# Segment 0 of an attention and MLP block attends whole: new buffers, split TensorE tasks and a new list of work

## The chip, the cores and the metric

One core of a Trainium2 chip runs the whole kernel as one launch. The metric is device microseconds of one execution, median of several. The core's engines run at the same time, each through its own list of instructions in order: TensorE (PE, matmuls and the loads of their weights), VectorE (DVE), ScalarE (ACT), GpSimd (POOL) and SyncE (SP, here the issue of DMAs). They wait for each other by semaphores. PSUM has eight banks of 512 f32 columns for 128 partitions; every matmul writes there and another engine must empty it.

## The reference, cut to what matters

2048 tokens of width 640, 32 heads of 20, four segments of 512 tokens, MLP width 1728. All inputs are bf16.

```python
q, k, v = heads of layernorm(x) @ wq, wk, wv
for s in range(4):                        # segments of 512 tokens
    p = softmax(qs @ ks.T * 20**-0.5 + causal mask)     # inside the segment alone
    a_dot = p @ vs
    a_mem = (phi(qs) @ M) / (phi(qs) @ z + 1e-6)        # phi(t) = t+1 if t>0 else exp(t)
    o = g * a_mem + (1 - g) * a_dot                     # g = sigmoid(beta), one per head
    M += phi(ks).T @ vs;  z += sum(phi(ks))
h  = x + o @ wo
h2 = h + silu(layernorm(h) @ w1) @ w2
```

In segment 0 the memory M is zero, so o is (1 - g) * a_dot there.

## The kernel before, in words

**One hand-written order.** `ORDER` is a list of 1371 task names. `schedule` (L287) walks it: each name may carry an engine (`/A` ACT, `/D` DVE, `/G` POOL, `/S` SP) and buffer slots (`:4`). Every engine executes its tasks in the order of the list; nothing is chosen at run time. A tracker (`Tracker.add`, L79, and `run`, L150) then puts semaphore waits where a task reads or overwrites what another engine wrote. A task whose name begins with `fill` puts so many 128x256 matmuls on zeros into PE's order (L598).

**The work of a segment s.** The names tell the task:

- `n1_st`, `n1_rs`, `n1_ap` (L706 to L723): statistics of a block of 128 tokens on DVE, the inverse deviation on POOL, the normalised block on DVE. In segment 0 the block is transposed by PE (`n1_tp` L732) and copied (`n1_te` L741), later by DMA (`n1_tr`).
- `v` (L774) and its eviction `ve`; `pr` (L808), Q and K of four heads at a time for all 512 tokens in five 128x512 matmuls, and its eviction `qe` (L816); `re_` (L677, L679) once copies wq and wk into the padded layout that `pr` reads. Heads 20 to 31 are spread over the pad rows, and `vt` DMAs gather them into QKV.
- `ex` and `ph` (L823 to L833): phi of Q and K.
- For each of eight groups of four heads: `qk` (L880), score products, four heads at once in four row tiles of 32; `e` (L891), exp of two banks, 128x1024, on ACT, from PSUM into a PT buffer; `mk` (L903), the causal mask of each diagonal block on POOL; `av` (L926), values, four heads at once in four column tiles; `oe`, `tn` (L955, L959), `nm`, `ad`: the memory's part, the transposition back, normalisation.
- `kt`, `mz` (L1048), `ma`, `mb`: the memory for the next segment.
- `ot` (a DMA transpose), `wo` (L1109), `rs`: output projection and residual; `n2_`: second layernorm; `h1` (L1143, the tail of 64 columns L1138), `th` (tanh, L1152), `s` (L1158); `h2` (L1178), `o` (L1195), `out`.

A group of score products covers 1280 columns per head: `a` (key block 0, 512 queries), `b` (blocks 1 and 3, 384 + 128), `e` (block 2 of two groups, 256 + 256). Segment 0 is cut differently: `x` tasks treat its queries 0 to 255 (256 + 128 columns) and `ya`, `yb` its queries 256 to 511, and `wo`, `h1`, `th` and `s` of its first two blocks run before those of the other two, with 256 columns a matmul.

**Buffers.** A `qk` task takes four neighbouring banks of PSUM, slot 0 or 4. PTA, PTB and PTE are pools of two buffers each. xT, hT and oT are one buffer each. Q and K of all segments share one tile QK, so that of segment 1 can be written only where that of segment 0 has been read.

Of the kernel before, what the change touches and what calls it, by code (L numbers as in the profile page):

```python
# [7 lines left out]
BF16 = mybir.dt.bfloat16  # L8
# [219 lines left out]
class Task:  # L228
    __slots__ = ("name", "engs", "emit", "reads", "writes", "prio", "mode", "allocs", "preds", "npred",
                 "succ", "ready", "lat", "start", "end", "eng", "idx", "bw")  # L230
# [4 lines left out]
class Graph:  # L235
# [15 lines left out]
    def task(self, name, engs, emit, reads=(), writes=(), prio=0.0, mode=None, reserve=(), lat=None, bw=0.0):  # L251

        t = Task()
        t.name, t.emit, t.mode, t.lat, t.bw = name, emit, mode, lat, bw
# [32 lines left out]
    def schedule(self):  # L287
# [3 lines left out]
        for row in ORDER:  # L291
# [3 lines left out]
            if name.startswith("fill"):  # L295
                o = owner["ps"][slots[0]]
                assert o is None or o.users == 0
                t = Task()
                a = Alloc("ps")
                a.slot = slots[0]  # L300
                t.name, t.eng, t.emit = "fill", PE, self.filler(a, int(name[4:]))
                order.append(t)
# [3 lines left out]
            t.eng = {"A": AC, "D": DV, "G": PO, "S": SP}[eng] if eng else list(t.engs)[0]  # L306
            assert t.eng in t.engs
# [41 lines left out]
WH = [(0, 0), (0, 1), (1, 0), (1, 1)]  # L349

# [20 lines left out]
n1_ap7:3 epsg1 oe4x/D:0 ve12/D kt02:0 n1_tr7 w_w1_2/S w_w2_0/S kt00:1 w_w1_3/S ex011:0 mk1yb mk5x mt0 qk6x0:4 av0y:2
e6x0:1 e6x2 tn4x:3 oe0y/D:0 av5x:0 tn3x:1 oe5x/A:1 qk7x0:4 e7x2:0 e7x0 nm4x:3 v10:2 nm3x:0 qk2ya0:4 ph041:2
n1_st10:2 ve10/D e2ya0:0 e2ya2 n1_rs11 mta2 mk7x n1_st9:3 n1_rs10 v13:0 mk6x tn0y:2 av7x:3 ve13/D nm0y:1 qk2yb0:4
oe7x/A:0 e2yb2:0 e2yb0 tn5x:3 tn7x:0 nm7x:2 av1y:1 av6x:2 qk3ya0:4 oe6x/D:1 nm5x:3 w_w1_4/S tn6x:2 nm6x:0 ot1:0
w_w2_5/S ot0 w_w2_4/S w_w2_1/S oe1y/A:0 e3ya0:1 e3ya2 ph011:1 pr101:1 mtb3 mz02:2 mk2yb av2y:3 qk3yb0:4 e3yb0:1
e3yb2 ma02/D:0 mz00:2 tn1y:0 oe2y/D:1 n1_ap11:1 qe101/D:0 pr100:3 qk4ya0:4 e4ya0:0 e4ya2 mk3yb ex031:2 nm1y:1
qe100/D wo1:0 av3y:3 qk4yb0:4 e4yb2:0 e4yb0 ma00/D:1 tn2y:2 ex101:1 rs1 wo0:0 oe3y/D:0 n2_st1:5 nm2y:2 kt04:0 tn3y:3
n2_rs1 nm3y:3 rs0 qk5ya0:4 pr140:2 n1_rs8 mk4yb pr121:3 e5ya0:1 e5ya2 qe140/A:0 qk5yb0:4 e5yb2:1 e5yb0 ex140:0
pr141:0 av4y:2 n2_ap1:0 n2_st0:4 n2_rs0 n2_ap0:2 kt01:1 n2_tr1:0 qk6ya0:4 qe141/D mk5yb pr120:1 ph031:0 oe4y/D:1
pr111:0 qe121/D:0 e6ya0:0 e6ya2 qk6yb0:4 qe120/D ex121:2 av5y:3 n2_tr0 h1_0_7_0:1 h1_0_0_0:2 e6yb2:0 e6yb0 qk7ya0:4  # L380
th0_7_0:0 ph101:2 qe111/D:0 oe5y/D:0 tn4y:0 s0_7_0:0 th0_0_0:1 h1_0_8_0:3 nm4y:0 s0_0_0 mz01:1 mz04:0 ma01/D:2
h1_0_3_0:2 e7ya2:1 e7ya0 th0_8_0:0 ma04/D:3 s0_8_0 th0_3_0:1 s0_3_0 tn5y:1 qk7yb0:4 e7yb2:1 mk6yb e7yb0 mk7yb mta0
av6y:0 mtb0 oe6y/A:1 h1_0_12_0:3 h1_0_1_0:2 qk8a0:4 th0_1_0:0 e8a2:0 e8a0 th0_12_0:1 s0_1_0 pr110:0 nm5y:1 qe110/D
h1_0_10_0:2 av7y:1 qk8e0:4 oe7y/D:0 th0_10_0:0 s0_12_0 pr130:0 s0_10_0 e8e2:0 e8e0 h1_0_5_0:2 h1_0_11_0:3 qk8b0:4
th0_5_0:1 n1_ap8:3 qe130/D:0 th0_11_0:0 w_w2_2/S kt03:1 tn7y:0 s0_5_0 nm7y:2 mz03:1 s0_11_0 h1_0_2_0:2 e8b2:0 e8b0
ma03/D:4 h1_0_6_0:0 th0_2_0:1 h1_0_13_0:1 th0_13_0:0 qk9a0:4 pr131:3 s0_2_0 s0_13_0 n1_ap10:0 h1_0_4_0:1 h1_0_9_0:2
qe131/D e9a2:1 e9a0 mk8a mk8e mm0 th0_6_0:1 th0_4_0:0 ex100:1 s0_6_0 mm4 mk8b mm6 qk9b0:4 vt19:0 th0_9_0:1 mm2 mm8
n1_rs9 mtb2 s0_4_0 w_w2_3/S vt16 vt10 vt18 e9b2:1 e9b0 av8:3 h2_0_0:0 h2_0_1 qk10a0:4 s0_9_0 ph100:0 ex141:1 ph121:1
e10a2:0 e10a0 h2_0_2 tn6y:2 h2_0_3 ph141:0 ex120:2 mk9a qk10b0:4 oe8/D:0 nm6y:3 o0 mzc0 mzc6 ph120:0 mzc2 h2_1_0:2
mk9b mm10 mzc4 e10b0:0 kt10:0 vt15 mm1 mzc1 mb00:0 e10b2 mk10a mzc5 mzc8 mm7 mzc7 mb03:0 mk10b ex111:1 n1_tr10:0  # L390
tn8:0 vt11 n1_tr8 nm8:0,0 h2_1_1 vt13 ot2 ot3 qk10e0:4 ph111:2 vt111 kt12:1 vt17 vt110 vt12 h2_1_2 av9:0 h2_1_3
ex110:2 ph110:0 oe9/D:1 e10e0:1 e10e2 qk11a0:4 mk10e mm3 mzc3 mb01:0 wo3:0 ad8:0 n1_ap9:2 o1 n1_tr9 vt14 e11a2:1
n1_tr11 e11a0 ex131:1 av10:2 mk11a mzc10 qk11b0:4 e11b0:1 e11b2 mk11b mb02:0 mm9 mzc9 rs3 oe10/D:0 tn9:0 wo2:2
qk12a0:4 nm9:1,1 v20:0 rs2 n2_st3:6 ex130:2 ph130:0 e12a2:0 e12a0 av11:2 qk13a0:4 n2_st2:7 mz12:3 ma12 ve20/A:0
e13a2:1 e13a0 v21:0 mz10:3 qk12b0:4 ve21/A e12b2:0 e12b0 ma10 tn10:0 pr210:3 n2_rs3 qk12e0:4 ph131:1 ad9 mm11 mzc11
mb04:0 mk13a n2_rs2 mk12b mk12a nm10:2,0 e12e2:0 pr220:0 n2_ap3:0 oe11/D:1 qe210/D:0 pr231:1 qe220/D:0 e12e0 mk12e
# [57 lines left out]
def build(nc, es, A_x, A_wq, A_wk, A_wv, A_wo, A_beta, B_x, B_w1, B_w2, out):  # L454
# [397 lines left out]
    def declare_ticks(s):  # L852
# [403 lines left out]
```

## Time and profile before

| | |
|---|---|
| median of three runs | 306.54 us (306.52 to 307.28) |
| span of the profiled execution | 305.4 us |
| busy PE, ACT, DVE, POOL | 291.0, 227.0, 218.7, 143.5 us |
| last matmul ends | 302.76 us |
| moved by DMA | 24.65 MB |

The page of the profile lists these for one execution. Lines that begin with an engine and a line of the kernel are groups: what is written and read, the shapes, how often, and the idle time of that engine before them with what ended it. A line of the timeline has the start, the duration, and then the group. A line of waits has who waited for whom, the total in us, how often, and the longest. A line of stages has the stretch, its length, and the busy time of PE, of PE's weight loads, of DVE, ACT and POOL (instructions in brackets), then granted clock, DMA share and GB/s.

### The profile page before, as it was taken

The page shows a single profiled execution, that of the slowest core. Times are in us where ns is not written, and L with a number is a line of the kernel's source. Part 1 is how long each engine was busy: PE and PEld are TensorE (multiplying, and loading weights), DVE is VectorE, ACT ScalarE, POOL GpSimd, SP SyncE. Part 2 cuts the span into 40 slices and gives each one's busy share as a digit, 9 for nine tenths or more (in the row PEclk, how much of TensorE's full clock was granted, in tenths as well). Part 3 has the DMA queues.
Part 4 walks back from the last instruction along what each step waited for, and adds up shares of the span by engine and source line. Part 5 has one row for each costly group of instructions (what it writes and reads, how often), then busy time and mean ns, then how long its engine had stood idle before and what let it go on. Part 6 is the DMA issues. An engine that isn't in the chain of part 4 may idle for free.

```text
span 305.4 us, 7240 instructions
## 1 busy us (share of the span) xinstructions
PE 291.0 (95%) x2876; PEld 166.5 (55%) x2900; DVE 218.7 (72%) x490; ACT 227.0 (74%) x322; POOL 143.5 (47%) x280
## 2 busy tenths in 40 slices
PE   8699898999999999999999999999999999999996
PEld 6434454555655445656654444556564466764574
DVE  5567999796788895877989878449776476934523
ACT  4488998999998979989889899978878951004410
POOL 4227754433687856536747419334973730300000
PEclk9899999999999999999999999999999999999999
DMA  6658468642264040055552400034250004242001
GB/s 197 211 195 239 75 166 223 127 97 42 90 105 80 17 62 2 1 91 76 114 146 63 67 17 19 2 64 69 39 108 2 0 2 88 64 88 86 0 24 64
DMA packets 48578, 24.65 MB, mean 81 GB/s; under 512 B 38881, under 2 KB 47457, under 8 KB 48545
## 3 DMA queue, kind: packets, MB, share of 16 engines
q1 hardware_dynamic: 47872, 23.09, 33.1%
q10 hardware_dynamic: 672, 1.10, 1.1%
q8 instruction: 23, 0.38, 0.5%
q14 instruction: 11, 0.08, 0.1%
HBM read 10.41 MB, written 2.62 MB: 43 GB/s over the span
## 4 chain that ended last, share of the span: by engine, by line
PE 72%; ACT 12%; DVE 7%; DMA 4%; issue 2%; POOL 1%; SPq 1%; DVEq 0%; ACTq 0%
PE ps_all L1178 18%; PE ps_all L1143 16%; PE ps_all L808 12%; PE ps_all L1109 7%; PE ps_all L880 6%; PE ps_all L926 5%; ACT PTA L891 4%; ACT PTB L891 3%; DMA sT<-in_A_wq_dram 3%; PE ps_all L774 2%; PE ps_all L955 2%; ACT PTE L891 2%; DMA oT<-otok 1%; PE ps_all L959 1%; PE ps_all L1048 1%
## 5 line engine op out<-in xcount | busy, mean ns | idle before, releaser
L891 ACT ACTIVATE PTA<-ps_all 128x1024 bf16<-128x1024 f32 x64 | 62.1, 1027 | 7.1 <-PE ps_all L880 6.5
L1178 PE MATMUL ps_all<-w_sb,sT 128*128 128x320 bf16 x448 | 65.2, 299 | 0.0
L891 ACT ACTIVATE PTB<-ps_all 128x1024 bf16<-128x1024 f32 (+1 forms) x64 | 58.9, 970 | 5.9 <-PE ps_all L880 5.6
L1143 PE MATMUL ps_all<-hT,w_sb 128*128 128x512 bf16 (+1 forms) x315 | 60.1, 335 | 0.9 <-issue 0.5
L1152 ACT ACTIVATE th<-ps_all 128x512 f32<-128x512 f32 (+2 forms) x70 | 34.0, 507 | 34.5 <-PE ps_all L1143 26.8
L1158 DVE SCALAR_TENSOR_TENSOR sT<-th,ps_all 128x512 bf16<-128x512 f32 (+2 forms) x70 | 38.0, 561 | 26.1 <-ACT th L1152 25.0
L903 POOL TENSOR_SCALAR_AFFINE_SELECT PTB<-PTB 128x512 bf16<-128x512 bf16 x64 | 41.2, 644 | 32.7 <-ACT PTB L891 30.4
L1178 PEld LDWEIGHTS ps_all<-w_sb,sT 128*128 128x128 bf16 x448 | 42.3, 98 | 19.3 <-issue 2.1
L1143 PEld LDWEIGHTS ps_all<-hT,w_sb 128*128 128x128 bf16 x325 | 30.3, 98 | 23.9 <-issue 1.3
L891 ACT ACTIVATE PTE<-ps_all 128x1024 bf16<-128x1024 f32 (+1 forms) x40 | 35.4, 943 | 2.2 <-PE ps_all L880 2.1
L903 POOL TENSOR_SCALAR_AFFINE_SELECT PTE<-PTE 128x512 bf16<-128x512 bf16 x40 | 25.9, 647 | 21.0 <-ACT PTE L891 19.5
L706 DVE BATCH_NORM_STATS2 stt<-x_tok 128x6 f32<-128x320 bf16 x64 | 27.9, 477 | 1.5 <-DMA x_tok<-in_A_x_dram 1.3
L808 PE MATMUL ps_all<-xT,wqr 128*128 128x512 bf16 x92 | 24.3, 391 | 3.2 <-ACT xT L741 2.4
L1109 PE MATMUL ps_all<-wo_sb,oT 128*128 128x320 bf16 x160 | 24.1, 299 | 1.0 <-DMA oT<-otok 0.7
L774 PE MATMUL ps_all<-wv_sb,xT 128*128 128x320 bf16 x160 | 24.3, 300 | 0.7 <-DMA xT<-xn_rot 0.5
L808 PE MATMUL ps_all<-xT,wkr 128*128 128x512 bf16 x94 | 24.0, 386 | 0.5 <-issue 0.3
L1000 POOL TENSOR_TENSOR otok<-on 128x320 bf16<-128x320 bf16 x24 | 19.0, 792 | 11.3 <-DVE on L992 11.3
L903 POOL TENSOR_SCALAR_AFFINE_SELECT PTA<-PTA 128x512 bf16<-128x512 bf16 x24 | 15.5, 645 | 16.6 <-ACT PTA L891 16.4
L1195 DVE SCALAR_TENSOR_TENSOR x_tok<-ps_all,x_tok 128x640 bf16<-128x640 f32 (+1 forms) x17 | 13.2, 780 | 14.1 <-PE ps_all L1178 14.0
L880 PE MATMUL ps_all<-QK 20*128 20x256 bf16 (+3 forms) x360 | 20.5, 286 | 1.7 <-ACT PTB L891 0.7
L992 DVE TENSOR_TENSOR on<-ps_all,rd 128x640 bf16<-128x640 f32 x24 | 19.8, 825 | 0.8
L817 DVE CAST QK<-ps_all 128x512 bf16<-128x512 f32 x24 | 16.3, 687 | 5.5 <-PE ps_all L808 5.1
(79 smaller groups left out, 403.5 us busy)
## 6 DMA issues: line engine op xcount, KB each, us to landing
out_dram<-x_tok SPq DMA_DIRECT2D x15, 160.0 KB, 1.9
w_sb<-in_B_w_dram SPq DMA_DIRECT2D x4, 432.0 KB, 5.8
w_sb<-in_B_w_dram SPq DMA_DIRECT2D x3, 480.0 KB, 4.3
x_tok<-in_A_x_dram SPq DMA_DIRECT2D x2, 640.0 KB, 4.7
QKV<-QK SPq DMA_DIRECT2D x16, 72.0 KB
wv_sb<-in_A_wv_dram SPq DMA_DIRECT2D x1, 800.0 KB, 4.9
sT<-in_A_wq_dram SPq DMA_DIRECT2D x1, 800.0 KB, 8.2
sT<-in_A_wk_dram SPq DMA_DIRECT2D x1, 800.0 KB, 9.9
```

The costliest lines, as they stand in the source:

```text
L706: T.add(DV, lambda e, hh=hh: e.bn_stats(out=stt[:, s, 6 * hh:6 * hh + 6], in_=xb[:, 320 * hh:320 * hh + 320]), reads=R((xa, xsub)), writes ...
L774: fns.append(lambda e, c=c, hh=hh: e.matmul(bank(ps, hh)[:, 0:320], lhsT=xT[:, c, 128 * i:128 * i + 128], rhs=wv_sb[:, c, 320 * hh:320 * h ...
L808: fns = [lambda e, kc=kc: e.matmul(bank(ps)[:, lo:hi], lhsT=wt[:, kc, c, :], rhs=xT[:, kc, lo:hi], start=(kc == 0), stop=(kc == NC - 1)) f ...
L880: fns.append(lambda e, j=j, o=o, r=r, q0=q0, q1=q1, qa=qa, ka=ka: e.matmul(ps_all[:, o:o + q1 - q0], lhsT=ka[32 * r:32 * r + DH, 128 * j:1 ...
L891: T.add(AC, lambda e: e.activation(out=pt[:, pta.slot, q0:q0 + 2, 0:width], in_=sc3[:, b0:b0 + 2, 0:width], func=ACT.Exp, scale=SCALE), re ...
L903: fns.append(lambda e, v=v: e.affine_select(out=v, in_=v, pattern=[[0, 4], [1, 128]], compare_op=ALU.is_ge, fill=0.0, base=0, channel_mult ...
L992: T.add(DV, lambda e: e.tensor_tensor(out=on[:, ona.slot, :, :].rearrange("p b (x e) -> p b x e", e=DH), in0=v[:, :, :, 0:DH], in1=r2.unsq ...
L1109: fns.append(lambda e, c=c, hh=hh: e.matmul(bank(ps, hh)[:, 0:320], lhsT=oT[:, c, 128 * i:128 * i + 128], rhs=wo_sb[:, c, 320 * hh:320 * h ...
L1143: fns = [lambda e, c=c: e.matmul(bank(ps)[:, lo:hi], lhsT=w1_sb[:, c, 128 * f:128 * f + 128], rhs=hT[:, c, lo:hi], start=(c == 0), stop=(c ...
L1152: T.add(AC, lambda e: e.activation(out=th[:, tha.slot, lo:hi], in_=bank(ps)[:, lo:hi], func=ACT.Tanh, scale=0.5), reads=R((ps, [0])), writ ...
L1158: T.add(DV, lambda e: e.scalar_tensor_tensor(out=sT[:, f, lo:hi], in0=th[:, tha.slot, lo:hi], scalar=1.0, in1=bank(ps)[:, lo:hi], op0=ALU. ...
L1178: fns.append(lambda e, f=f, t0=t0, fr=fr, hh=hh: e.matmul(bank(ps, hh)[:, 0:320], lhsT=sT[:, f, t0:t0 + 128], rhs=w2_sb[:, fr, 320 * hh:32 ...
```

## The change

The whole list is new. Beside it:

- Segment 0 has `a`, `b` and `e` score tasks like the other segments, one `av`, `oe`, `tn` and `nm` per group, and one set of `h1`, `th` and `s` for its 512 tokens.
- A `qk` task takes two pairs of banks, each anywhere in PSUM.
- One pool PT of seven buffers stands for PTA, PTB and PTE; one pool T of three for xT, hT and oT.
- Q and K of segment 0 lie in the space of w2 (rows 0 to 7 of `w2_sb`), so that parts 0 to 2 of w2 are loaded only after they have been read.
- `v`, `wo`, `pr` and `h1` are two tasks each (`.0` and `.1`); `ph` is `pa` and `pb`. `re_` may run on POOL.
- A PE task could also run as four column tiles of 32 (`/C`); no entry of the list asks for it. The tail of `h1` is always in four tiles of 32 columns.

The diff, cut:

```diff
-        "x": 12, "xn": 4, "xT": 1, "hT": 1, "wq": 1, "wk": 1, "wv": 1, "wo": 1, "w1": 1, "w2": 1,
+        "x": 12, "xn": 4, "T": 3, "wq": 1, "wk": 1, "wv": 1, "wo": 1, "w1": 1, "w2": 1,
+        "QZ0": 1, "QZ1": 1, "QZ2": 1, "QZ3": 1, "QZ4": 1,
-        "PTA": 2, "PTB": 2, "PTE": 2, "oTs": 2, "on": 2, "rd": 4, "otok": 1, "oT": 1,
+        "PT": 7, "oTs": 2, "on": 2, "rd": 4, "otok": 1,
...
+    QK0 = w2_sb[:, 0:8, :].rearrange("p f e -> p (f e)").rearrange("p (c w t) -> p c w t", c=5, w=2)
...
+    def mms(eng, out, lhsT, rhs, start, stop):
+        if eng != "cols":
+            return [lambda e: e.matmul(out, lhsT=lhsT, rhs=rhs, start=start, stop=stop)]
+        return [lambda e, p=p: e.matmul(out[p:p + 32, :], lhsT=lhsT[:, p:p + 32], rhs=rhs, start=start, stop=stop,
+                                        tile_position=(0, p)) for p in (0, 32, 64, 96)]
...
-            G.task(f"re_{k}{c}", {DV: 0.36 if c < 3 else 0.42, AC: 0.72}, emit, rr, ww, prio + c)
+            G.task(f"re_{k}{c}", {DV: 0.36 if c < 3 else 0.42, AC: 0.72, PO: 0.8 if c < 3 else 0.9}, emit, rr, ww, prio + c)
...
-                sca = G.alloc("ps", nr)
+                sca = [G.alloc("ps", 2) for _ in range(nr // 2)]
...
-        if s == 0:
-            for g in range(NG):
-                k = P["x0"] + P["xs"] * g
-                pe = scores(f"{g}x", "PTE", PTE, [(g, 0, 0, 256, 0), (g, 1, 128, 256, 256)], k, 384,
-                            [(0, 0), (1, 0)])
...
+        pe = None
+        for g in range(NG):
+            k = k0 + g
+            pa = scores(f"{k}a", "PT", PT, [(g, 0, 0, L, 0)], k)
+            pb = scores(f"{k}b", "PT", PT, [(g, 1, 128, L, 0), (g, 3, 384, L, 384)], k + P["qkp"])
...
-        parts = [(0, 2), (2, 4)] if s == 0 else [(0, 4)]
+        parts = [(0, 4)]
...
+    def load_w2():
+        for k, (f0, f1) in enumerate(((0, 4), (4, 7), (7, 10), (10, 13))):
+            old = [(a, WH) for a in segs[0]["qk"]] if k < 3 else []
+            load_w(f"w2_{k}", w2_sb[:, f0:f1, :], cw(B_w2[128 * f0:128 * f1, :]), 2 + k, 0.45 * (f1 - f0),
+                   [(W["w2"], [k])] + old)
```

The head of the two lists:

```diff
-n1_rs1 epsg0 n1_ap0:0 fill21:0 n1_tp0:0 n1_te0/A:0 n1_ap1:1 fill6:2 n1_tp1:2 n1_te1/A v00:0 v01:2 n1_st2:2 n1_rs2
-n1_st3:3 n1_rs3 mt1 mt2 mta1 n1_ap2:2 n1_ap3:3 n1_tp2:4 n1_te2/D re_wq1/A:0 fill4:6 n1_tp3:6 n1_te3/A pr010:6
+n1_st1:6 n1_rs1 sel n1_ap0:3 mtb1 fill42:0 n1_tp0:3 n1_ap1:3 fill5:0 n1_tp1:6 w_k n1_st2:4 n1_rs2 n1_te0/A:1 n1_st3:0
+beta n1_rs3 re_wq3/G:0 v00.0:0 v00.1 n1_ap2:3 n1_te1/A v01.0:6 ve00/A:0 mm1 mm5 fill3:4 n1_tp2:2 re_wk1/G:0 n1_te2/A
+v01.1 n1_ap3:1 n1_tp3:0 v02.0:4 v02.1 n1_te3/A re_wq0/D pr000.0:0 pr000.1 ve02/A v03.0:3 re_wk0/D mt2 re_wq4/A
```

More of the change, by code (lines that the diff above doesn't have):

```diff
@@ L229 @@
     __slots__ = ("name", "engs", "emit", "reads", "writes", "prio", "mode", "allocs", "preds", "npred",
[L230 removed]
+                 "succ", "ready", "lat", "start", "end", "eng", "idx", "bw", "cols", "alt")
 class Graph:
@@ L305, in schedule @@
             assert not any(self.tasks[p].name in todo for p in t.preds), name
-            t.eng = {"A": AC, "D": DV, "G": PO, "S": SP}[eng] if eng else list(t.engs)[0]
-            assert t.eng in t.engs
+            t.cols = eng == "C"
+            t.eng = {"A": AC, "D": DV, "G": PO, "S": SP, "C": PE}[eng] if eng else list(t.engs)[0]
+            assert t.eng in t.engs and (t.alt or not t.cols)
             for a in t.allocs:
@@ L822, in e_ex @@
                     def e_ex(eng, c=c, w=w, exa=exa, wall=wall):
-                        T.add(AC, lambda e: e.activation(out=ex[:, exa.slot, :], in_=QK[:, c, w, :], func=ACT.Exp),
+                        T.add(AC, lambda e: e.activation(out=ex[:, exa.slot, :], in_=qkt[:, c, w, :], func=ACT.Exp),
                               reads=R((qk[c], wall)), writes=R((exa, [0])))
```

375 lines of the change are left out of this document (185 added, 190 removed).

## The prediction

> **What bounds the kernel now.** I read the page's busy table and its slices first.
>
> ```profile
> PE 291.0 (95%) x2876; PEld 166.5 (55%) x2900; DVE 218.7 (72%) x490; ACT 227.0 (74%) x322; POOL 143.5 (47%) x280
> ...
> PE   8699898999999999999999999999999999999996
> ...
> ACT  4488998999998979989889899978878951004410
> ...
> PEclk9899999999999999999999999999999999999999
> ```
>
> TensorE (PE) is busy in 291.0 of 305.4 us, so there are three ways to gain: less PE work, fewer waits of PE, a better start. ScalarE (ACT) is nearly as full until about slice 31. Then the timeline of PE, which starts each group of matmuls:
>
> ```profile
> 1.12 4.66 PE L599 MATMUL ps_all<-zpad 128*128 128x256 bf16 x21 [1.12 <-DVE zpad L578]
> 5.69 0.72 PE L732 MATMUL ps_all<-ident,xn_rot 128*128 128x128 bf16 x5
> 6.20 0.91 PE L599 MATMUL ps_all<-zpad 128*128 128x256 bf16 x6
> ...
> 13.77 1.91 PE L808 MATMUL ps_all<-xT,wqr 128*128 128x512 bf16 x4 [2.38 <-ACT xT L741]
> 15.48 2.89 PE L808 MATMUL ps_all<-xT,wkr 128*128 128x512 bf16 x10
> 18.30 0.34 PE L880 MATMUL ps_all<-QK 20*128 20x256 bf16 x8
> 18.57 1.25 PE L808 MATMUL ps_all<-xT,wqr 128*128 128x512 bf16 x5
> 19.66 1.24 PE L808 MATMUL ps_all<-xT,wkr 128*128 128x512 bf16 x5
> 20.84 0.34 PE L880 MATMUL ps_all<-QK 20*128 20x256 bf16 x8
> 21.11 1.25 PE L808 MATMUL ps_all<-xT,wqr 128*128 128x512 bf16 x5
> ```
>
> Starts tell what a group costs. Five 512-column matmuls take 1.09 us from start to start (18.57 to 19.66), a plain stream of 0.216 us each. From 19.66 to 20.84 it is 1.18, and the eight score products behind take 0.27 where their two rounds of 256 and 128 columns are 0.165 at that rate. So each change between full-array matmuls and matmuls in row or column tiles costs PE about 0.10 us. Elsewhere single matmuls start 0.136 us apart at 320 columns, 0.109 at 256, 0.056 at 128. The start is slow: 21 fillers take 0.213 us each, half speed, the clock is full from 6.4 us, PE idles 2.38 us, and then seven projection matmuls run at half speed again.
>
> The waits of PE, and the stages, with busy times:
>
> ```profile
> PE ps_all L808 <- ACT xT L741: 2.4, 1, 2.4
> ...
> PE ps_all L880 <- ACT PTB L891: 0.7, 2, 0.5
> PE ps_all L1109 <- DMA oT<-otok: 0.7, 1, 0.7
> PE ps_all L926 <- POOL PTB L903: 0.6, 1, 0.6
> ...
> 18.30:71.00 52.70, 49.28 (x605) 26.13 (x609) 43.70 (x118) 49.08 (x72) 27.23 (x55) 1.00 0.60 153
> 71.00:127.00 56.00, 54.32 (x620) 30.92 (x625) 44.47 (x100) 52.08 (x73) 37.74 (x78) 1.00 0.28 52
> ```
>
> No single wait is large after the start. The stages are cut at the first score product (18.3), the first of segment 1 (71.0, qk8a0) and of segment 2 (127.0, qk16a0).
>
> **PE's work, counted.** I took the PE order of both built programs and priced each matmul (one round of four tiles counts once) by its start-to-start time, and each change of tiling by 0.10:
>
> - before: 261.8 us of stream, 217 changes; after: 263.8 us, 199 changes.
> - Stream: 61 fillers instead of 41, +2.2. The rest falls by 0.2: h1 of segment 0 has 65 products of 512 columns for 130 of 256. Score and value columns are the same (1280 per group and product kind), only in fewer, wider groups; the tail of h1 keeps its columns. Its tiles are 32 columns wide instead of 64: L926 already runs four such tiles in a round, so 0, within 0.1 us either way for all tails.
> - Changes of tiling: 18 fewer, -1.8.
>
> Splitting PE tasks in two, the free choice of PSUM pairs, seven shared PT buffers, three shared T buffers and Q/K of segment 0 in w2's space add no instruction; they act through waits. The split of phi in two tasks keeps both VectorE (DVE) operations.
>
> **The start.** Before, real work by 18.3 us is 20 v matmuls (2.7), 15 projections (3.2) and transposes (1.1). After, the list puts all 40 v matmuls there (5.4), 10 projections (2.2) and the transposes: 8.7 instead of 7.1. When does its first score start? The 42 fillers begin at 1.12; 24 at 0.213 to 6.3 us, 18 at 0.109: they end at 8.2. Before, the transpose could start at 5.69. It matters here because ap1 now writes the same xn buffer (3) as ap0 and so waits on DVE for the first transpose; behind it on DVE stand the statistics of blocks 2 and 3. From 8.2, with the durations of before: transpose to 8.5, ap1 to 9.2, statistics of blocks 2 and 3 to 11.35 (two times 1.05), rstd on GpSimd (POOL), ap3 to 12.9, fourth transpose to 13.2, v02 to 14.6, then pr000, half of v03, pr001 and the other half to 18.1, the eviction, and the first score at 18.4. So 1.6 us more work done 0.1 later: **-1.5**. The 2.4 us idle and the second half-speed stretch go; 2.5 us of that are eaten by the fillers. Bounds: fillers all at half speed end at 10.1 (+1.9 on this); at best the first transpose starts where it did, at 5.69 (-2.5).
>
> Here a rule bears on it. The trace went to full clock 5.2 us after the first matmul. The Trainium skill, "TensorE: Matmul & The Clock Gate", Part 1, puts the warm-up at a time budget of about 3.4 us in a free-running window, not a number of matmuls; by it the fillers would end near 7.4, an estimate, and the sum would be 0.8 lower. It also puts the fall back to half rate after an idle window of that length, while this trace shows it after 2.38 us; there the measurement decides.
>
> Five weight rearrangements move to POOL. No row shows them; the nearest are L1084 (168 to 252 elements, 179 ns more: 2.1 ns an element, 1.35 us for 640) and DVE's own copies (0.36 us). I take 1.35, the row on the same engine. wk lands at about 14.1, so re_wk1 ends at 15.5, and its projection comes only after the first score at 18.4. This 3 us of cover makes it 0; without it the cost would be up to 1 us.
>
> **After the start: waits.** Own execution before: 18.3 to the first score; PE work 47.6, 53.7 and 172.3 in the three stages; the last matmul ends at 302.76, the span 2.65 later. So waits are 305.4 - 2.65 - 18.3 - 273.6 = 10.9: 5.1, 2.3 and 3.5 by stage. For other engines I multiplied the instructions that the list has in a stage by their start-to-start times (exp of 1024: 0.905; ex 0.52; th 0.494; evictions 0.49 to 0.74; mask 0.594):
>
> - first score to qk8a0: before PE 47.6, ACT 46.7, DVE 42.0, POOL 27.9; after **PE 38.0, ACT 40.3, DVE 37.6**, POOL 30.0
> - to qk16a0: before 53.7, 49.3, 41.1; after 52.0, 49.1, 42.8
> - to the end: before 172.3, 110.7; after 180.2, 105.5.
>
> So the new list runs segment 0 with three engines level. Cut finer (some 20 pieces between score products), the fullest engine exceeds PE by 5.5 us in sum, where before it was 4.1: +1.4. Against it, score products before used banks 4 to 7 alone until segment 2 and could start only when both exps of the last had ended; a new one needs only two free pairs, so PE can refill one pair while ACT reads another. PE's waits for exps (L891) in the list of waits come to 1.7, most of it there. I set the two against each other: **0**, with -5.4 (waits only where another engine is fuller) and +5 as ends.
>
> Loads of w2: parts 0 to 2 wait until Q/K of segment 0 are read, and parts 1 and 2 each for the landing of the part before, on SP. At 5.8 us each they land by about 121 us, and h2_0_2 stands near 127: covered. Behind them on SP stands kt20, with some 2 us to spare; gone, that costs 1 to 2 us, inside the +5.
>
> **Sum** on the span: 18.4 + 38.0 + 52.0 + 180.2 + 10.9 + 2.65 = 302.1, that is -3.3 (1.5 from the start, 2.0 from stream and changes, less 0.1 for one later filler and rounding). The median lies 1.1 above the span, so 306.5 - 3.3 = **303.2 us**.
>
> **Rivals.**
>
> - *ACT becomes the bound of the first 90 us.* Before, ACT stood idle 52.7 - 46.7 = 6.0 us in the first stage and 56.0 - 49.3 = 6.7 in the second. If it still idles so long, the stages last 40.3 + 6.0 and 49.1 + 6.7, PE waits 12.1 there instead of 7.4, and the time is 303.2 + 4.7 = 307.9: slower. For it: ACT alone exceeds PE in stage one. Against: the looser pairs. My forecast has ACT idle 8.0 us in both stages; from 11.3 on the gain is gone.
> - *The loose buffers do all they can*: waits fall to the 5.5 us of unequal load: 303.2 - 5.4 = 297.8. Against: semaphore latencies remain.
> - *The fillers eat the start* (the change does not bring its earlier start): all 42 at half speed, 305.1.
> - *The clock rises earlier*: if it is full after 16 fillers of 0.213 us instead of 24, the other 26 at 0.109 end at 7.4: 302.4. The trace's 5.2 us speak against it. The rule of the Trainium skill named above is this case.
>
> **Chances.** Forecast 0.38, ACT the bound 0.27, loose buffers 0.15, fillers 0.10, earlier clock 0.10. A measurement of this kernel tells about 0.3% (0.9 us) from no change. Faster: 0.31 + 0.15 + 0.06 + 0.08 = 0.60; within: 0.07 + 0.05 + 0.04 + 0.02 = 0.18; slower: 0.22, all from ACT. The range runs from 299.5 to 308.5: it leaves out half of the loose-buffer case and the worst of ACT's. The sign of faster holds most of the chance; its own range is 300.5 to 305.5.
>
> **What would show it.** In the profile after: the filler group from 1.12 to about 8.2 and the first score near 18.4 (the start); no half-speed projections around 14 us; PE's waits for exps small and its waits between first score and qk16a0 near 7.4; starts of segment 1 and 2 near 61.5 and 116; ACT idle 8 us in these stages. Wrong would be: many waits of score products for ACT or of value products for POOL in the first 110 us, ACT idle there 11 us or more, or long waits for transposes in the last 170.

## The result and the profile after

| | before | after |
|---|---|---|
| median, seven runs each | 305.82 us (304.96 to 307.28) | 303.46 us (301.99 to 304.82) |
| span of the profiled execution | 305.4 us | 301.8 us (time 303.53) |
| first score product | 18.3 | 17.96 us |
| first score product of segment 1, of segment 2 | 71.0, 127.0 | 61.2, 115.4 us |
| last matmul ends | 302.76 | 298.89 us |
| waits of PE by stage (stage less counted PE work) | 5.1, 2.3, 3.5 | 5.2, 2.2, 3.3 us |

The ratio is 0.992, 95% interval 0.990 to 0.994: faster by 0.8%. The span of the profiled execution is 3.6 us shorter. The ratios of three experiments below (x2 and x3 first; both; both sets of fillers) leave out executions over 1.5% longer than the fastest of the same kernel, and in the first and the last of them the profiled execution is such a one.

The page of the changed kernel, the lines that stand first in the prediction:

```profile
PE 291.5 (97%) x2757; PEld 158.8 (53%) x2757; DVE 222.8 (74%) x465; ACT 213.6 (71%) x275; POOL 148.3 (49%) x292
...
PE   8999789999999999999999999999999999999996
...
ACT  3589898999899999966769967868888741004400
...
PEclk9999999999999999999999999999999999999999
```

PE is as busy as before in a shorter span. The 6 that PE had from 7.6 to 15.3 us is gone; one thin place is left, a 7 and an 8 between 30 and 45 us. The timeline of PE at the start:

```profile
1.13 6.38 PE L614 MATMUL ps_all<-zpad 128*128 128x256 bf16 x42 [1.13 <-DVE zpad L593]
7.34 0.44 PE L745 MATMUL ps_all<-ident,xn_rot 128*128 128x128 bf16 x5
...
14.27 1.24 PE L544 MATMUL ps_all<-tT,wqr 128*128 128x512 bf16 x5
15.35 0.84 PE L544 MATMUL ps_all<-wv_sb,tT 128*128 128x320 bf16 x5
...
17.96 0.40 PE L899 MATMUL ps_all<-w_sb 20*128 20x512 bf16 x4
```

The fillers end at 7.3, no projection runs at half speed (five in 1.08 us, 14.27 to 15.35), and there is no idle time of 2.4 us. The longest waits of PE, and the stages cut at the same events as before (the last row runs 0.3 us beyond the last matmul):

```profile
PE ps_all L899 <- DVE otok L995: 1.1, 2, 0.9
...
PE ps_all L544 <- DMA tT<-otok: 0.7, 1, 0.7
...
PE ps_all L980 <- DVE oTs L962: 0.5, 1, 0.5
PE ps_all L947 <- DVE Mz L1085: 0.5, 1, 0.5
PE ps_all L980 <- ACT PT L912: 0.4, 1, 0.4
```

```profile
17.96:61.20 43.24, 39.47 (x415) 17.51 (x415) 39.75 (x92) 40.99 (x50) 31.41 (x70) 1.00 0.58 142
61.20:115.40 54.20, 53.26 (x532) 26.04 (x532) 46.19 (x96) 51.16 (x65) 31.63 (x59) 1.00 0.42 93
115.40:299.20 183.80, 182.28 (x1699) 103.82 (x1698) 126.95 (x251) 112.69 (x148) 75.12 (x127) 1.00 0.24 51
```

The order of the list is new: VectorE stands at its head, and no score product waits long for an exp (L912). In the first stage DVE is busy 39.75 of 43.24 us, ACT 40.99, PE 39.47. With the counted work of ACT (40.3 and 49.1) it idles 2.9 and 5.1 us in the first two stages, together 8.0.

### The profile page after: what moved, and what is told of

It reads as the page before. It is cut to its first block, busy times and chain, and to the rows that moved or that the text cites. A ratio compares the mean times of both kernels' runs of the same rounds, so it can differ in the third digit from the quotient of the medians.

```text
span 301.8 us, 6943 instructions
## 1 busy us (share of the span) xinstructions
PE 291.5 (97%) x2757; PEld 158.8 (53%) x2757; DVE 222.8 (74%) x465; ACT 213.6 (71%) x275; POOL 148.3 (49%) x292
## 4 chain that ended last, share of the span: by engine, by line
PE 76%; DVE 10%; DMA 5%; ACT 2%; SPq 2%; issue 2%; POOL 1%; DVEq 0%
PE ps_all L544 58%; PE ps_all L899 7%; PE ps_all L947 5%; DMA x_tok<-in_A_x_dram 2%; DVE stt L719 2%; PE ps_all L976 2%; ACT PT L912 2%; DMA tT<-otok 2%; PE ps_all L980 2%; DMA tT<-xn_rot 1%; PE ps_all L1056 1%; SPq L1109 1%; DVE w_sb L830 1%; PE ps_all L1146 1%; DVE xn_rot L736 1%
## 5 line engine op out<-in xcount | busy, mean ns | idle before, releaser
L912 ACT ACTIVATE PT<-ps_all 128x1024 bf16<-128x1024 f32 x160 | 154.4, 1031 | 24.9 <-PE ps_all L899 23.3
L924 POOL TENSOR_SCALAR_AFFINE_SELECT PT<-PT 128x512 bf16<-128x512 bf16 x128 | 82.3, 648 | 70.7 <-ACT PT L912 67.1
L544 PE MATMUL ps_all<-w_sb,sT 128*128 128x320 bf16 x448 | 65.7, 299 | 0.1
L544 PE MATMUL ps_all<-tT,w_sb 128*128 128x512 bf16 x260 | 62.6, 380 | 0.3 <-issue 0.3
L1159 ACT ACTIVATE th<-ps_all 128x512 f32<-128x512 f32 (+1 forms) x56 | 31.7, 587 | 37.2 <-PE ps_all L544 26.9
L544 PEld LDWEIGHTS ps_all<-w_sb,sT 128*128 128x128 bf16 x448 | 42.6, 98 | 19.7 <-issue 2.4
L1165 DVE SCALAR_TENSOR_TENSOR sT<-th,ps_all 128x512 bf16<-128x512 f32 (+1 forms) x56 | 36.4, 663 | 20.7 <-ACT th L1159 20.4
L544 PEld LDWEIGHTS ps_all<-tT,w_sb 128*128 128x128 bf16 x260 | 23.2, 98 | 27.6 <-issue 3.6
L544 PE MATMUL ps_all<-tT,wqr 128*128 128x512 bf16 x100 | 25.8, 381 | 0.5 <-DMA tT<-xn_rot 0.5
L544 PE MATMUL ps_all<-tT,wkr 128*128 128x512 bf16 x100 | 25.3, 380 | 0.0
L544 PE MATMUL ps_all<-wv_sb,tT 128*128 128x320 bf16 x160 | 24.9, 299 | 0.0
L544 PE MATMUL ps_all<-wo_sb,tT 128*128 128x320 bf16 x160 | 23.8, 299 | 0.7 <-DMA tT<-otok 0.7
L728 POOL TENSOR_TENSOR rst<-mvt,eps_c 128x1 f32<-128x1 f32 x32 | 6.7, 210 | 28.5 <-DVE mvt L722 28.4
L730 POOL TENSOR_TENSOR rst<-rst,eps_c 128x1 f32<-128x1 f32 x32 | 18.3, 572 | 2.5
L544 PEld LDWEIGHTS ps_all<-wo_sb,tT 128*128 128x128 bf16 x160 | 15.0, 98 | 7.8 <-issue 1.1
```

Source lines behind the costliest of these rows:

```text
L544: return [lambda e: e.matmul(out, lhsT=lhsT, rhs=rhs, start=start, stop=stop)]
L912: T.add(AC, lambda e: e.activation(out=pt[:, pta.slot, q0:q0 + 2, 0:width], in_=sc3[:, b0:b0 + 2, 0:width], func=ACT.Exp, scale=SCALE), re ...
L924: fns.append(lambda e, v=v: e.affine_select(out=v, in_=v, pattern=[[0, 4], [1, 128]], compare_op=ALU.is_ge, fill=0.0, base=0, channel_mult ...
L1159: T.add(AC, lambda e: e.activation(out=th[:, tha.slot, lo:hi], in_=bank(ps)[:, lo:hi], func=ACT.Tanh, scale=0.5), reads=R((ps, [0])), writ ...
L1165: T.add(DV, lambda e: e.scalar_tensor_tensor(out=sT[:, f, lo:hi], in0=th[:, tha.slot, lo:hi], scalar=1.0, in1=bank(ps)[:, lo:hi], op0=ALU. ...
```

## Experiments

The theory after the result: the gain is PE's smaller work and the fuller start, and the waits stay equal only because the loose pairs pay for running three engines level. What is left is (a) the fillers and the landing of x2 at the start and (b) VectorE's lateness from 28 to 37 us. The rivals: other engines are as full in (b), or the clock decides.

**The changed kernel once more**

> The changed kernel once more, unaltered, on the chip of the next three runs, so that they can be compared with it. Every theory expects a ratio to the kernel before of 0.992 within 0.002, a span near 301.8 us and the first score product near 18.0 us.

Median 303.85 us, ratio 0.9932 (0.9908 to 0.9955), first score 18.49, span 302.1. One thing differs from the first profile. A table by stretch (its last columns are granted clock, DMA share, GB/s), first of this execution, then of the first one:

```profile
33.00:37.00 4.00, 2.33 (x43) 1.24 (x36) 3.70 (x12) 3.49 (x5) 1.70 (x4) 1.00 0.37 73
37.00:41.00 4.00, 4.00 (x31) 2.04 (x33) 2.63 (x7) 3.34 (x5) 3.59 (x9) 0.57 0.39 81
```

```profile
33.00:37.00 4.00, 2.33 (x31) 1.35 (x30) 3.47 (x12) 3.49 (x5) 2.24 (x5) 1.00 0.33 62
37.00:41.00 4.00, 3.80 (x48) 2.09 (x46) 3.93 (x11) 3.83 (x5) 3.58 (x9) 1.00 0.39 82
```

PE works 2.33 of the 4 us from 33 to 37 in both. In the one, the clock then falls to 0.57; five value projections take 1.39 us instead of 0.84. By the mean clock of each execution (0.994 against 0.999 or 1.0), 8 of 12 executions of the changed kernel have such a fall, and 2 of 17 of the kernel before that were run beside this one. The last section shows what differs between the two. The means are 303.9 us for those 8 and 302.9 for the other 4: about 1 us.

**Half of the fillers**

```diff
-mtb1 fill42:0 n1_tp0:3
+mtb1 fill21:0 n1_tp0:3
```

> Only edit: 21 fillers instead of 42 ahead of the first transpose. Theory: the fillers cost the start nothing, because in the changed kernel VectorE takes up the statistics of block 2 only at 8.73 us, when the DMA of x2 has landed, and that DMA does not know of the fillers. Then the first score product stays within 0.4 us of 17.96, the ratio within 0.002 of the unaltered changed kernel, and if the clock falls in the longer idle time the start is even up to 1 us later. Rival (the prediction's own chain, in which the transposes wait for the fillers and everything behind them waits for the transposes): the fillers end about 2 us earlier, and the first score comes 1 to 2 us earlier, the span 1 to 2 us shorter.

```profile
1.13 3.78 PE L614 MATMUL ps_all<-zpad 128*128 128x256 bf16 x21 [1.13 <-DVE zpad L593]
5.59 0.45 PE L745 MATMUL ps_all<-ident,xn_rot 128*128 128x128 bf16 x5 [0.68 <-DVE xn_rot L736]
...
6.97 0.89 DVE L719 BATCH_NORM_STATS2 stt<-x_tok 128x6 f32<-128x320 bf16 x2 [0.33 <-DMA x_tok<-in_A_x_dram]
...
16.20 0.40 PE L899 MATMUL ps_all<-w_sb 20*128 20x512 bf16 x4
```

Theory and rival each hold in part. In the 11 profiles with this order of work at the start the first score comes 9.22 or 9.23 us after VectorE takes up the statistics of block 2. These start at the later of two events: the landing of x2, and the end of the second normalised block, which waits for the first transpose and so for the fillers. In this run the landing decides (6.95 us). In the unaltered run beside it x2 has landed at 8.42, and VectorE is held by the transpose:

```profile
8.90 0.45 DVE L736 TENSOR_SCALAR xn_rot<-x_tok,mvt,rst 128x640 bf16<-128x640 bf16 x1 [3.21 <-PE ps_all L745]
9.26 0.88 DVE L719 BATCH_NORM_STATS2 stt<-x_tok 128x6 f32<-128x320 bf16 x2
```

So of the 2.3 us between the two first scores (16.20 and 18.49) 0.8 are the fillers' and 1.5 an earlier landing. In the first profile x2 landed at 8.70 and the fillers cost nothing, as the theory says; over the nine profiles with 42 fillers they hold the statistics 0 to 2.0 us beyond the landing, 0.8 in the mean. In all three profiles with 21 fillers the landing decides: 6.95, 7.81 and 8.91 us, and first scores at 16.20, 17.06 and 18.16. The 2.3 us hold up to segment 1 (60.01 against 62.34); 1.46 are left at segment 2 and at the last matmul. Ratio 0.9902 (0.9871 to 0.9933): 0.3% below the unaltered kernel, with intervals that overlap, so a gain is not shown.

**x2 and x3 ahead of wv**

```diff
-x1:1 w_wv:0 halfc x2:2 x3:3 w_q:0
+x1:1 halfc x2:2 x3:3 w_wv:0 w_q:0
-fill42:0 n1_tp0:3 n1_ap1:3
+fill21:0 n1_tp0:3 n1_ap1:0
```

> Three edits at the start: 21 fillers instead of 42, a buffer of its own for the second normalised block (no wait for the first transpose), and the loads of x2 and x3 issued ahead of that of wv. Theory: the landing of x2 at 8.7 us ends the chain in front of the first score; issued ahead of the 800 KB of wv it lands 2 to 3 us earlier, the statistics of blocks 2 and 3 follow block 1 on VectorE at once, and the first score moves from 17.96 towards 16.5, where the landing of wk at 13.6 holds it (wk's landing, rearrangement, five projection products 1.25, eviction 0.6): a span 1 to 1.5 us shorter, a ratio 0.003 to 0.005 lower than that of the unaltered changed kernel. Rival A: the 13.6 us of wk alone set the start, or the stage behind is held by VectorE and takes the gain back: within 0.5 us. Rival B: the fillers were what held it: then the run with 21 fillers alone has the same gain.

```profile
10.42 4.16 PE L544 MATMUL ps_all<-wv_sb,tT 128*128 128x320 bf16 x15 [3.16 <-DMA wv_sb<-in_A_wv_dram]
14.37 0.85 PE L614 MATMUL ps_all<-zpad 128*128 128x256 bf16 x3
```

A miss that the theory had not named. The statistics of block 2 do follow at once (6.66), but wv is now what lands last: PE waits 3.16 us for it, the clock falls, and 15 value projections take 4.0 us from start to start instead of 2.0. The first score comes at 21.95. Ratio 0.9945 (0.9915 to 0.9975), executions from 301.8 to 308.2 us; the profiled one, at 308.19, is among the longest, and the shortest has a mean clock of 1.0 against its 0.983.

**Statistics of segment 2 later**

```diff
-n1_st9 n1_rs9 (behind e3a0)  n1_st11 (behind ma02)  n1_st10 (behind e4b2)
+n1_st9 n1_rs9 n1_st11 n1_st10 (all behind qk5a0)
```

> Only edit: the statistics of blocks 9, 10 and 11 (three times 1.05 us on VectorE) stand behind qk5a0 in the list instead of ahead of it. Theory: PE's waits from 21 to 41 us come from VectorE, which carries more than PE there (the chain of waits runs over VectorE from 21.7 to 40.6 us); with some 3 us less of work ahead of 41 us PE waits 1.5 to 2.5 us less in the first stage, segment 1 begins at 59 to 60 instead of 61.2, and the span is 1 to 2.5 us shorter. Rival 1 (the prediction's): exp on ScalarE is the bound there; then nothing moves, within 0.4 us. Rival 2: the time is only moved, and VectorE is late in the second half of the stage instead: segment 1 begins within 0.5 us of 61.2.

Slower, 1.0086 (1.0062 to 1.011), where 1 to 2.5 us of gain were expected. Up to qk4a0 nothing moves (41.62 against 41.55): the statistics of block 9 stood behind 37 us, so the edit took nothing from the stretch in which DVE is late. Then qk5a0 to qk6a0 take 3.4 us longer. The timeline of POOL and PE's list of waits from 18 to 63 us show why:

```profile
49.41 0.19 POOL L728 TENSOR_TENSOR rst<-mvt,eps_c 128x1 f32<-128x1 f32 x1 [4.25 <-DVE mvt L722]
49.67 0.55 POOL L730 TENSOR_TENSOR rst<-rst,eps_c 128x1 f32<-128x1 f32 x1
50.19 1.34 POOL L924 TENSOR_SCALAR_AFFINE_SELECT PT<-PT 128x512 bf16<-128x512 bf16 x2
```

```profile
PE ps_all L947 <- POOL PT L924: 3.3, 1, 3.3
```

POOL takes the inverse deviation of block 9 in the list's order, waits 4.25 us for its statistics, and the masks queued behind it are late for the value products. The moved step's second instruction, on another engine, is the larger part of the cost. A second fall of the clock, from 54.4 to 57.9 us, lies in the piece behind it, qk6a0 to qk7a0, which takes 7.7 us instead of 6.35.

**VectorE relieved in the right place**

```diff
-n1_st7 (behind pr030.0)  n1_rs7 n1_ap7 (behind oe0)  n1_st6 n1_rs6 (behind e2e0)
+n1_st7 (behind nm1)  n1_rs7 n1_st6 (behind e3a0)  n1_ap7 n1_rs6 (behind e3b0)
-n1_ap6 (behind e3b0)  n1_st9 n1_rs9 (behind e3a0)  n1_st11 (behind ma02)  n1_st10 (behind e4b2)
+n1_ap6 (behind ve10)  n1_st9 (behind ma02)  n1_rs9 (behind ve11)  n1_st11 (behind e4b2)  n1_st10 (behind qe110)
```

> Edit: the statistics of blocks 7, 6, 9, 11 and 10 on VectorE are each put one place later in the list (block 7 behind the second normalisation of segment 0, block 6 where block 9 was, and so on, block 10 behind the eviction of the second projection of segment 1), and the inverse deviations on GpSimd and the normalised blocks with them, each behind its own statistics and ahead of nothing that waits longer. So VectorE has 2.1 us less to do ahead of 36 us. Theory: PE waits for VectorE between 28 and 37 us (0.3, 0.3, 0.9 and 0.5 us in the list of waits, and half the stretch from 33 to 37 idle); it reaches qk4a0 1.5 to 2.5 us earlier, and the granted clock does not fall behind the waits (0.57 of full at 37 to 41 us in the unaltered changed kernel of these runs), 1.3 us more: segment 1 begins at 59 to 60.5 instead of 62.3, the span is 1.5 to 3.5 us shorter. Rival 1: ScalarE is as full there, nothing moves before qk4a0 (within 0.5 us). Rival 2: what is gained is lost between qk4a0 and qk8a0, where the statistics now stand, on VectorE or by masks on GpSimd that queue behind the inverse deviations: segment 1 begins within 0.5 us of 62.3 or later.

Ratio 0.9999 (0.9974 to 1.0025). From qk2a0 to qk3a0 it takes 6.39 us instead of 7.25, so VectorE did hold PE there, by 0.9 and not by 2. From qk4a0 to qk5a0 it takes 8.92 instead of 5.86. The chain of waits from 30 us on and the longest wait of PE:

```profile
30.82 1.88 ACT PT L912 x2
32.75 1.95 ACT PT L912 x2
34.75 0.64 POOL PT L924
35.45 1.23 POOL PT L924 x2
...
41.76 0.55 POOL rst L730
42.31 1.39 POOL PT L924 x2
43.75 0.64 POOL PT L924
```

```profile
PE ps_all L947 <- POOL PT L924: 1.7, 1, 1.7
```

With VectorE lighter, the chain runs over four exps and then the masks of POOL; then POOL again waits for the moved statistics. Nor does the clock stay up, as was expected: 11 of 12 executions have 0.994, and in the profiled one it is at 0.50 from 45.0 to 48.4 us, inside the piece that takes 8.92. How much of the 3.1 us more is the masks' and how much the clock's was not taken apart. Rivals 1 and 2 both hold in part: DVE, ACT and POOL are all nearly full in segment 0, and relieving one of them in this way gave 0.9 us, which was lost behind it.

**Both**

> The same edit, and 21 fillers instead of 42. If the start and the stretch from 28 to 37 us are separate costs, the gains add: first score near 16.2, segment 1 at 57 to 58.5, a span of 298 to 299.5 us, a ratio to the kernel before near 0.98 to 0.985. Rival: the gain of the start is what runs into VectorE's late stretch, and the sum is no better than the better of the two alone (span 300.6 for the fewer fillers).

Ratio 1.0005 (0.9987 to 1.0023): no better than the relief alone (0.9999), and worse than the fewer fillers alone (0.9902). That is the rival's outcome, and more. The first score is at 17.06, segment 1 at 61.65.

**Value projections of blocks 2 and 3 later**

```diff
-v02.0:4 v02.1 (behind n1_tp3)  ve02/A v03.0:3 (behind pr000.1)  v03.1 (behind qe001)  ve03/D
+v02.0:2 v02.1 ve02/A v03.0:2 v03.1 ve03/D (all behind pr041.1)
```

> Only edit: the value projections of blocks 2 and 3 (20 matmuls of 320 columns, 2.7 us of PE, and one eviction each on ScalarE and VectorE) stand after the projections of segment 0, behind pr041.1, instead of ahead of the first score product. Theory of the prediction (the 1.6 us of extra work that PE does in the time in which it would wait anyway are a gain of the start): the first score comes only 0.5 to 1.5 us earlier than 18.0 to 18.5, since the landing of wk and the eviction behind it hold it, the 2.7 us come later on PE, and the span is 1 to 2 us longer than that of the unaltered changed kernel (302.1). Rival: behind the first score VectorE is late and PE waits for it, so that work put there is hidden in those waits: the span stays within 0.5 us, or is shorter by the earlier first score.

Ratio 1.0008 (0.9982 to 1.0035), that is 0.76% or 2.3 us above the unaltered kernel; first score 17.59, 0.9 us earlier; qk2a0 at 32.50, 3.8 later. PE's waits name ACT Vx L796 with 0.8 and DVE Vx L797 with 0.9: both projections are put into one bank here, so the second waits for the first one's eviction, and the score product behind it for the second one's. Up to 1.7 of the 2.3 us are thus the edit's own. Work that was in the start costs time behind the first score: that is the theory's direction. The size of the credit, 1.6 in the sum, is not shown by this run.

**The loose pairs alone taken back**

```diff
-                    T.run(PE, fns, R(*ra), R(*scw))
+                    T.run(PE, fns, R(*ra), R(*scw), after=[("exps", 0)])
```

> Only edit: each score task waits until both exps of the score task before it have ended; that is what the four neighbouring banks of the kernel before imposed, and so the edit takes back the loose pairs alone. Theory: the loose pairs are what lets three engines run level in segments 0 and 1; without them ScalarE waits for PE and PE for ScalarE in turn at each of the 80 score tasks or so, 0.1 to 0.3 us each in the first 115 us, and the span is 4 to 10 us longer, with waits of score products for exp at the head of PE's list of waits. Rival: the list is written so that the exps of the last score task have ended in any case: less than 1 us.

The edit makes a score task wait for every exp that the list has ahead of it; 12 of the 79 later score tasks stand ahead of an exp of the task before and are held less. The largest effect of the study: ratio 1.0411 (1.0382 to 1.044), 318.15 us, 14.7 us above the unaltered changed kernel, and slower than the kernel before. Segment 2 begins at 127.5 instead of 116.4.

```profile
PE ps_all L899 <- ACT PT L912: 13.3, 22, 1.5
```

22 waits of score products for exps make 13.3 us, 9.0 of them ahead of segment 1; in the changed kernel none of this kind stands in the list. This prices the loose pairs for a list that was written with them; the only list here that was written for four neighbouring banks is that of the kernel before.

**The price of a change of tiling**

55 extra matmuls of 64 columns on zeros, in a row tile or over the full array, ahead of 55 full-array tasks behind qk20a0:

```diff
+lambda e: e.matmul(bank(a)[:, 0:64], lhsT=zpad[0:20, 0:128], rhs=zpad[0:20, 0:64], ..., tile_position=(0, 0))
```

> Edit: 55 extra matmuls on zeros, of 20 rows and 64 columns in a row tile, each between two full-array tasks of TensorE behind qk20a0 (where PE waits least), each into a bank that the task behind it overwrites. So 110 changes of tiling more, and 55 times 0.03 us of stream. Theory (0.10 us of PE per change): 55 times 0.03 plus 110 times 0.10 is 12.6 us; 10 to 13 us longer than the unaltered changed kernel. Rival 1: the 0.10 us is only the latency from one matmul to the next where the operands differ, not the tiling: then as much longer as the run with full-array matmuls. Rival 2: PE has 4 us of waits in this part that hide some of it: 6 to 9 us.

> The control to the run with row tiles: the same 55 extra matmuls at the same places, 64 columns, but with all 128 rows and no tile position, so no change of tiling. Theory: 55 times 0.03 us, 1.6 us longer than the unaltered changed kernel (within 1 us). Rival: each extra instruction costs as much as in the row tiles (10 us or more).

Ratios 1.0306 (1.0268 to 1.0343) and 1.0011 (0.9988 to 1.0033). From qk20a0 to the start of the last matmul it takes 151.9 us in the unaltered run (152.7 in the first profile), 154.9 with the full-array ones, 164.5 with the row tiles: 2.3 to 3.0 us for 55 instructions, and 9.6 us for 110 changes, **0.087 us** each. By the ratios it is 9.0 us and 0.082 each. Rival 1 is out: the control with the same instructions lacks these 9 us. The timelines, row tiles first:

```profile
169.85 0.32 PE L981 MATMUL ps_all<-ident,oTs 128*128 128x84 bf16 x4
170.11 0.20 PE L615 MATMUL ps_all<-zpad 20*128 20x64 bf16 x1
170.24 1.25 PE L544 MATMUL ps_all<-tT,w_sb 128*128 128x512 bf16 x5
```

```profile
170.27 0.32 PE L981 MATMUL ps_all<-ident,oTs 128*128 128x84 bf16 x4
170.46 0.20 PE L615 MATMUL ps_all<-zpad 128*128 128x64 bf16 x1
170.50 1.24 PE L544 MATMUL ps_all<-tT,w_sb 128*128 128x512 bf16 x5
```

Read starts, not durations: from the transposition to the tasks behind the extra matmul 0.39 us in tiles, 0.23 without: 0.16 for two changes.

**More fillers where PE waits**

```diff
-fill3:1 qk3a0:4,1 oe1/D:0 tn1:7
+fill10:1 qk3a0:4,1 oe1/D:0 fill4:7 tn1:7
```

> Only edit to the changed kernel: 11 more matmuls on zeros of 256 columns where PE waits for VectorE around 35 us, 7 ahead of the score product that waited 0.94 us and 4 ahead of the transposition that waited 0.50 us; at 0.109 us each they fit into these waits. Theory: in most executions of the changed kernel these two waits are followed by some 3.4 us at half clock (granted clock 0.994 of the execution instead of 1.0), which costs 1.3 to 1.6 us; with PE kept busy the clock does not fall, the executions have 0.999 or 1.0, and their median is 0.8 to 1.5 us below that of the unaltered changed kernel (ratio to the kernel before 0.988 to 0.991 instead of 0.993). Rival 1: the clock falls for another reason (at a set time, or by the chip's state): the 0.994 stay, and the time within 0.4 us. Rival 2: the fillers are late themselves and hold the score product: up to 1 us longer.

All ten executions have a mean clock of 0.999 or 1.0 (8 of 12 had 0.994 without). The two waits shrink to 0.17 and none, and qk3a0 and tn1 start where they did. First the changed kernel (its first profile), then this run:

```profile
35.42 0.39 PE L899 MATMUL ps_all<-w_sb 20*128 20x512 bf16 x4 [0.94 <-DVE otok L995]
36.32 0.33 PE L980 MATMUL ps_all<-ident,oTs 128*128 128x84 bf16 x4 [0.50 <-DVE oTs L962]
```

```profile
34.01 1.25 PE L614 MATMUL ps_all<-zpad 128*128 128x256 bf16 x10
35.43 0.39 PE L899 MATMUL ps_all<-w_sb 20*128 20x512 bf16 x4 [0.17 <-DVE otok L995]
35.76 0.61 PE L614 MATMUL ps_all<-zpad 128*128 128x256 bf16 x4
36.33 0.33 PE L980 MATMUL ps_all<-ident,oTs 128*128 128x84 bf16 x4
```

So it is PE's sparse stretch that lets the clock fall. These executions ran on another chip, without unaltered ones of the changed kernel beside them, and the chip would be a rival; the busy shares in the last section speak against it. A gain in time is not shown: 303.63 us median, ratio 0.992 (0.9893 to 0.9948) against 0.9932, that is 0.4 us and within the intervals, where 0.8 to 1.5 were expected. These executions are 0.8 us longer (means) than the four of the changed kernel without a fall; what takes that is open. In its profile one wait of 0.9 us ahead of a task of L544 between 161 and 183 us, without a releaser, is not in the first profile, but one execution does not carry a cause.

**Both sets of fillers**

> The same, and 21 fillers instead of 42 at the start. If the two are separate costs, both gains are there: a first score near 16.2, no stretch at half clock behind 33 us, a span of 298.5 to 300 us, a ratio to the kernel before of 0.980 to 0.986, and so a version faster than both kernels. Rival: with fewer fillers at the start the clock falls elsewhere in the first 20 us or the start's gain is lost in the stages behind, as half of it was in the run with 21 fillers alone: a span of 300.5 or more.

Median 302.5 us, ratio 0.9875 (0.9831 to 0.9919): the fastest kernel here, 1.2% below the kernel before. Over the changed kernel (0.992, 0.9932) it is 0.5% by the ratios, and the intervals overlap. Five of six executions have full clock. The profiled one, the longest at 306.13, shows no fall near 37 us but one from 90.5 to 93.9, and its first score comes at 18.16 instead of the expected 16.2, since x2 landed at 8.91: that the gains of the two sets add is not shown.

## Why the prediction was right, point by point

- **The sum.** Forecast -3.3 on the span, measured -3.6. The direction and the size were right; the agreement to 0.3 us is partly luck, since the two profiled executions differ in clock. That of the kernel before has a mean granted clock of 0.994, from the stretch at half speed between 13.2 and 16.6 us, while 63 of its 74 executions beside the experiments have 0.999 or 1.0; that of the changed kernel has 0.999. Executions at full clock differ by 2.8 us in the mean (305.7, 15 of the 17, against 302.9, 4 of the 12), executions with a fall by 3.6 (307.5 against 303.9). The medians of the seven side by side differ by 2.4, as the changed kernel falls more often, which the prediction did not know. The median was also set only 1.1 us above the span; in the profiled execution of the changed kernel it is 1.7 (303.53 and 301.8).
- **The start** (-1.5, first score 18.4). Measured 17.96, and 17.3 to 18.6 in the later profiles with 42 fillers. From the end of the second normalised block to the first score the chain was right: 9.2 us forecast, 9.22 or 9.23 measured. What sets it going was half right. The landing of x2 is not in the forecast's chain, and in the first profile (8.70 us) it came last; in seven of the nine profiles with 42 fillers the fillers did. So the fillers do not eat 2.5 us, but 0 to 2.0. The -1.5 itself holds only against an execution of the kernel before that has the stretch at half speed: its seven projections take about 1.5 us more there than at 0.216 us each, and 63 of 74 executions have no such fall. Against those the start gains about nothing, an estimate, as no trace of one was kept; what then remains of the sum is the -2.0 of stream and changes, where 2.8 was measured at full clock. Where the other 0.8 comes from is open. The clock's rise was mis-sized too: the fillers were set to end at 8.2 with full clock 5.2 us after the first matmul; across the 14 profiles it is full 2.7 to 5.7 us after it, and the transpose behind 42 fillers starts between 7.1 and 8.5. The earlier-clock rival is thus no other case but one end of what every execution draws. The Trainium skill, "TensorE: Matmul & The Clock Gate", Part 1, says that the window is free-running and the warm-up differs from run to run; the trace agrees, with a spread of 3 us rather than the half microsecond either way that it names.
- **Stream and changes of tiling** (-0.2 and -1.8). A change costs 0.08 to 0.09, not 0.10: 18 fewer give 1.5. The stream was counted and not tested by a run of its own.
- **The moved rearrangements** (0, taken at 1.35 us each). POOL takes 0.85 to 1.08 for one of the five; re_wk1 ends at 14.55, and the projection that reads it comes behind the first score: the cover was there.
- **Waits** (0 net, ends -5.4 and +5). Right in size, 10.7 against 10.9 (with 0.087 for a change of tiling in both counts, each is some 2.7 higher). That something large stood against the level load is shown: taking back the loose pairs alone costs 14.7 us. That is almost three times the bound of +5, so this list without them is slower than the kernel before. One premise was slightly off: a score task of segment 0 (`qk0ya0`) did use banks 0 to 3 before. The loose-buffer rival, waits of 5.5, did not come.
- **ACT as the bound** (rival, 0.27). It did not come: ACT idles 8.0 us in two stages, as forecast; over the whole kernel it waits for PE's score products (23.3 of its 24.9 idle us before exps), not PE for it. Where PE does wait in segment 0 it is for VectorE, to which the prediction gave 37.6 us of work and no rival. VectorE is busy 39.75 there.
- **Fillers eat the start** (rival, 0.10): none of the profiles has all 42 at half speed (13 to 27 slow ones ahead of the rise). What the fillers hold back, 0.8 us in the mean, is less than the forecast's sum had allowed for.

## What to carry to other kernels

When a change loads several engines level, look for what lets them overlap; here the freedom of PSUM pairs was worth 14.7 us to this list although no row of the old profile priced it, and relieving one of the level engines gave 0.9 us and then met the next. A step that is moved takes along its instructions on other engines: one small instruction, put ahead of what it waits for, holds all that is queued behind it. Before a step is credited with a gain, look at what else its successor waits for: the fillers held the start in some executions and a DMA in others. Judge a median by several executions and their granted clock before a term of 1 us is believed, and ask first whether the profiled execution is a usual one.

## What the runs showed of the hardware that was not expected

- The clock needs no long idle time to fall, and it falls on a grid. In the 13 profiles that hold changes of the granted clock, each of 13 falls comes a whole number of times 3.41 us after the first rise to full clock, and the slow stretch lasts 3.41 us, in three of them 6.83. In the 3.41 us ahead of each fall PE is busy 1.2 to 1.9 us; in all other such pieces ahead of the kernel's end it is busy 1.84 or more. This would explain why 8 of 12 executions of the changed kernel fall and 4 do not; one of each kind was profiled. In the unaltered run (first line) the sparse part, with single gaps of at most 0.94 us, lies in one piece, and the clock falls at its end; in the first profile (two lines) the border of two pieces lies inside it:

```profile
33.77:37.18 3.41, 1.74 (x25) 1.04 (x22) 2.97 (x10) 2.90 (x4) 1.88 (x4) 1.00 0.36 69
```

```profile
31.78:35.20 3.42, 2.48 (x42) 1.44 (x39) 3.32 (x11) 3.42 (x4) 0.74 (x3) 1.00 0.47 79
35.20:38.61 3.41, 2.49 (x27) 1.35 (x28) 2.92 (x9) 2.73 (x4) 2.98 (x7) 1.00 0.30 58
```

With the eleven fillers PE is busy 3.02 and 3.21 us in the two pieces there. In the kernel before the piece with the gap of 2.38 us, ahead of the fall at 13.2, has PE busy for 1.48. The Trainium skill, "TensorE: Matmul & The Clock Gate", Part 1, names an idle window of about 3.4 us for the fall; the length of the slow stretch and the grid agree with that, the idle time does not, as PE was busy for a third to over a half of the window ahead of each fall.
- VectorE can slow down beside GpSimd. The same operation, in 0.29 us while POOL is idle (32.4 to 32.9 us) and in 0.71 while POOL is busy throughout (27.8 to 28.5). Over the 14 profiles it takes 0.28 to 0.29 in all 132 places with POOL idle; of 110 with POOL busy throughout about half take no longer than that, the others 0.30 to 0.77. So none is slow without POOL, and a busy POOL does not make every one slow:

```profile
27.82 0.71 DVE L843 TENSOR_SCALAR phiK<-w_sb 128x512 bf16<-128x512 bf16 x1
...
32.49 0.29 DVE L843 TENSOR_SCALAR phiK<-w_sb 128x512 bf16<-128x512 bf16 x1
```

The Trainium skill, "SBUF — State Buffer", "SBUF: two separate sides", has the two engines share one pair of ports under an exclusive lock; the rows are in keeping with it. Segment 0, which holds masks, inverse deviations and copies on POOL, is where this falls on an engine that PE waits for; what it costs the kernel was not measured.
